# A third accumulator buffer in the gate stages, and GpSimd products moved one stage earlier, in a hashed attention followed by a gated MLP

## The chip, the core and the metric

The kernel runs on one core of one Trainium2 chip. The core has a matrix engine (TensorE, here PE, with its weight loads PEld), a vector engine (VectorE, DVE), an activation engine (ScalarE, ACT), GpSimd (POOL) and a queue engine (SyncE, SP) that issues most DMAs. All of them share the on-chip memory SBUF; PE writes its results to eight accumulator banks (PSUM), from which DVE and ACT read. The metric is the time of one execution in microseconds (us), lower is better.

## The reference

Four batches of eight heads, 768 positions of 64 numbers. Each query and key row gets a bucket: the signs of six projections. Attention is taken only between rows of the same bucket. The result, as 3,072 tokens of 512 numbers, goes through a gated MLP with a gated residual.

```python
q_bits = (np.einsum('bhsd,dk->bhsk', q, proj) > 0)          # 6 bits; k likewise
mask = q_bucket[:, :, :, None] == k_bucket[:, :, None, :]
scores = np.where(mask, scale * q @ k.T, -1e9)
attn = softmax(scores) @ v                                  # then x: 3072 x 512
g = x @ w_gate;  val = x @ w_val                            # 512 -> 1536
ffn_out = gelu(g) * val @ w_out                             # 1536 -> 512
out = x + sigmoid(x @ w_res) * ffn_out
```

## The kernel before

The work is staged by batch. An attention stage of batch b ("a0" to "a3") handles its four pairs of heads (pairs 4b to 4b + 3) in 36 slots, nine a pair. In a slot PE computes 1,024 columns of scores into a two-bank buffer `sp` (L500), ACT takes the exponential `e` (L511), and two slots later PE multiplies the values (L475). In a1 to a3 the MLP of the batch before runs between: residual gate `rps` (L557, then `th` on ACT, L561) in bank `r`, and the output `fps` (L571, then two DVE instructions, L574 and L577, and a store) in bank `f`, six token tiles of 16 matmuls each.

Between two attention stages stands a gate stage ("g0" to "g3"): twelve blocks m, in each of which PE computes the gate half and the value half, eight matmuls each, into one `sp` buffer each (L525). ACT takes the gelu of the first (`gt`, L542), and DVE multiplies it by the second into `hh` (L545). There are two `sp` buffers, so a buffer comes back after two halves. The banks `r` and `f` hold nothing of the gate stage: `hs` (hash sums) uses `r` at its start, and the projection's results use both in the attention stages.

The mask is built without comparing: `nat` holds, for each row of q and k, its 64 numbers (the cast, L261 to L265) and six bits as ±0.5 (L305 or L344). It is transposed into `aug`, by PE in the beginning and by a DMA transposition of SP later (`turn`, L360), so that one matmul gives score and bits together. The bits come in one of two ways. By hash: DVE transposes blocks of 32 (`tr`, L273), PE multiplies by the projection into `hs` (L284), DVE transposes back (L292 into bank `f`, or L296 into SBUF as `ht`), and `bits` compares with zero, four instructions on DVE or POOL. By sums: POOL multiplies the rows by one projection column, one half of a pair at a time (`product`, L335, 12 for each of q and k of a pair), DVE adds up each (`add_up`, L341), and POOL compares (`bits_sums`, L344). Product buffers are shared: in gate stages with `th` (two buffers), in attention stages with `gt` (two buffers).

Every engine works its own list strictly in order. The order comes from lists in the code. `PLAN` lists a0's steps; in the slots of a1 to a3 and after the blocks of the gate stages, pieces hang at places: `('a', b, slot)` or `('g', b, block)`. `PLACES` gives the place of each product; the sum of the product two before stands just ahead of it; `LAYS` gives the place of `bits_sums` and the transposition. Pairs 10, 11, 14 and 15 go by sums, with products from a1 on; 4 to 9, 12 and 13 by hash. At a pair's head a preset matmul (L450) and a DVE copy (`repeat`, L454) initialise the accumulator `av`, and after its last value the `finish` (L419, L420) makes `x_tok`. `x_sb` is its transposition, on which the next gate stage's matmuls work; for the last pair of a batch it is issued (L428) at the very end of the attention stage.

Of the kernel before, what the change touches and what calls it, by code (L numbers as in the profile page):

```python
# [29 lines left out]
    ('vs', 0), ('load', 4, 0), ('load', 5, 1), ('load', 4, 1), ('load_v', 3),  # L30
# [57 lines left out]
XDMA = 2
# [4 lines left out]
def kernel(  # L93
# [12 lines left out]
    nc = tc.nc  # L106
# [14 lines left out]

    LDX, TRX, CSX = 9, 26, 26
    LDY = {1: [('a', 1, 0), ('a', 1, 0), ('a', 1, 3), ('a', 1, 1)], 2: [('a', 2, 0), ('a', 2, 2), ('a', 2, 19), ('a', 2, 19)]}
    CSY = [(5, 's'), (5, 's'), (10, 's'), (10, 's')]
    PLACES = {1: [('a', 1, 9), ('a', 1, 10), ('a', 1, 10), ('a', 1, 11), ('a', 1, 13), ('a', 1, 15), ('a', 1, 15), ('a', 1, 16), ('a', 1, 17), ('a', 1, 18), ('a', 1, 18), ('a', 1, 21), ('a', 1, 22), ('a', 1, 23), ('a', 1, 24), ('a', 1, 26), ('a', 1, 27), ('a', 1, 30), ('a', 1, 34), ('g', 1, 0), ('g', 1, 0), ('g', 1, 0), ('g', 1, 1), ('g', 1, 2), ('g', 1, 3), ('g', 1, 3), ('g', 1, 4), ('g', 1, 5), ('g', 1, 5), ('g', 1, 6), ('g', 1, 6), ('g', 1, 7), ('g', 1, 7), ('g', 1, 8), ('g', 1, 8), ('g', 1, 9), ('g', 1, 9), ('g', 1, 10), ('g', 1, 10), ('g', 1, 11), ('a', 2, 2), ('a', 2, 3), ('a', 2, 5), ('a', 2, 6), ('a', 2, 8), ('a', 2, 9), ('a', 2, 13), ('a', 2, 14)], 2: [('a', 2, 1), ('a', 2, 2), ('a', 2, 13), ('a', 2, 14), ('a', 2, 16), ('a', 2, 18), ('a', 2, 19), ('a', 2, 23), ('a', 2, 24), ('a', 2, 24), ('a', 2, 26), ('a', 2, 31), ('a', 2, 32), ('a', 2, 33), ('g', 2, 0), ('g', 2, 0), ('g', 2, 0), ('g', 2, 0), ('g', 2, 1), ('g', 2, 2), ('g', 2, 3), ('g', 2, 3), ('g', 2, 4), ('g', 2, 5), ('g', 2, 5), ('g', 2, 6), ('g', 2, 6), ('g', 2, 7), ('g', 2, 8), ('g', 2, 8), ('g', 2, 9), ('g', 2, 9), ('g', 2, 10), ('g', 2, 10), ('a', 3, 0), ('a', 3, 4), ('a', 3, 4), ('a', 3, 4), ('a', 3, 6), ('a', 3, 7), ('a', 3, 8), ('a', 3, 13), ('a', 3, 13), ('a', 3, 14), ('a', 3, 14), ('a', 3, 15), ('a', 3, 15), ('a', 3, 16)]}
    DRAIN = {1: ('a', 2, 16), 2: ('a', 3, 20)}
    LAYS = {1: [('g', 1, 7), ('g', 1, 8), ('a', 2, 5), ('a', 2, 17)], 2: [('g', 2, 7), ('g', 2, 8), ('a', 3, 6), ('a', 3, 21)]}
    PRS = (1, 8)  # L130
    NE = 9
    C = 2048.0
    ALPHA = C / np.sqrt(D)
# [196 lines left out]
    def product(x, n, tag):  # L330
        bit, hi = divmod(n, 2)
        if x not in sums:
            sums[x] = hh_pool.tile([P, HT, NBITS], FP32, tag=f"sums{x[0] % 2}{x[1]}", name="sums")
# [460 lines left out]
```

## Time and profile before

| | us |
|---|---|
| median of 3 runs (lowest, highest) | 339.43 (339.25, 339.55) |
| the profiled execution's own time | 339.34 |
| its span, first to last instruction | 337.3 |
| a0 (start to the first gate matmul) | 0 to 45.2 |
| g0 | 45.2 to 78.7 |
| a1 | 78.7 to 121.8, with gate block 0 begun to 126.5 |
| g1 | 126.5 to 157.4 |
| a2, g2, a3, g3 and the last projection | to 205.2, 235.9, 284.3, 313.3, 337.3 |

Times in the rows are counted from the span's start. A row of the timeline gives start, length, engine, line, operation, tiles, shapes and count; in brackets stands the idle time before it and what ended it. A row of the groups gives busy time, mean in nanoseconds, then idle time before and its releasers. A row of waits gives total, times and longest. Rows of engines that end in q are of their queue. Consecutive instructions of one engine overlap a little, so that their starts tell more than their lengths.

### The profile page before, as it was taken

To read this page: it belongs to the slowest core of one execution; us is meant where nothing else is said; L and a number is where in the kernel's file an instruction comes from. 1 tells how busy PE (TensorE), PEld (TensorE's weight loads), DVE (VectorE), ACT (ScalarE), POOL (GpSimd) and SP (SyncE) were. 2 spreads that over 40 slices of the span, in tenths; PEclk is the share of its full clock that TensorE was granted. 3 is DMA by queue.
4 is the path that set the end of the run, shared out by engine and by line. 5 is a ranking of instruction groups with operands and counts; after the bars stand their busy time and mean duration, and the time that the engine had idled before them with its cause. 6 is when DMAs were issued, how large, how long until landed. Compare 5 with 4: busy or idle time off the path is not lost.

```text
span 337.3 us, 7740 instructions
## 1 busy us (share of the span) xinstructions
PE 332.4 (99%) x3086; PEld 204.0 (60%) x3086; DVE 216.3 (64%) x458; ACT 213.8 (63%) x247; POOL 175.0 (52%) x260
## 2 busy tenths in 40 slices
PE   8999999999999999999999999999999999999996
PEld 7767665565666655565666665665566665666444
DVE  7977575554577958876577896876577444343243
ACT  4889962337999952437999982255999984322220
POOL 4779920235299943578799972567879100000000
PEclk9999999999999999999999999999999999999999
DMA  7998999999965223518068933825050340000012
GB/s 228 370 289 125 217 242 202 179 166 205 313 222 149 72 85 81 109 32 187 3 167 229 273 92 94 134 47 96 1 126 33 80 101 33 31 2 0 31 64 94
DMA packets 74387, 43.88 MB, mean 130 GB/s; under 512 B 52544, under 2 KB 71360, under 8 KB 74352
## 3 DMA queue, kind: packets, MB, share of 16 engines
q1 hardware_dynamic: 67872, 37.95, 45.3%
q0 software_dynamic: 6400, 5.44, 10.7%
q8 instruction: 24, 0.39, 0.5%
q14 instruction: 11, 0.09, 0.1%
q10 hardware_dynamic: 80, 0.00, 0.0%
HBM read 29.56 MB, written 6.29 MB: 106 GB/s over the span
## 4 chain that ended last, share of the span: by engine, by line
PE 83%; POOL 8%; ACT 4%; DVE 3%; issue 1%; DMA 1%; POOLq 0%; DVEq 0%; ACTq 0%
PE sp L525 37%; PE fps L571 14%; PE sp L500 14%; PE av L475 7%; PE rps L557 5%; POOL pr L335 4%; PE hs L284 3%; ACT ering L511 3%; ACT e L511 1%; PE wps L229 1%; PE pt L373 1%; POOL v L394 1%; DMA x_sb<-x_tok 1%; DVE sums L341 1%; POOL va L386 1%
## 5 line engine op out<-in xcount | busy, mean ns | idle before, releaser
L511 ACT ACTIVATE e<-sp 128x1024 bf16<-128x1024 f32 x117 | 117.7, 1027 | 8.6 <-PE sp L500 3.7
L335 POOL TENSOR_TENSOR pr<-ld,projr 128x384 f32<-128x384 f32 x96 | 93.8, 998 | 47.0 <-DVE sums L341 31.9
L542 ACT ACTIVATE gt<-sp 128x768 bf16<-128x768 f32 x48 | 38.9, 810 | 83.7 <-PE sp L525 80.0
L500 PE MATMUL sp<-aug,aug 71*128 71x256 bf16 (+1 forms) x384 | 86.0, 325 | 0.5
L571 PE MATMUL fps<-wo,hh 128*128 128x512 bf16 (+2 forms) x312 | 79.6, 362 | 0.0
L545 DVE TENSOR_TENSOR hh<-gt,sp 128x768 bf16<-128x768 bf16 x48 | 45.8, 954 | 42.9 <-PE sp L525 39.5
L525 PE MATMUL sp<-x_sb,wg 128*128 128x512 bf16 (+1 forms) x384 | 70.9, 326 | 0.0
L525 PE MATMUL sp<-x_sb,wv 128*128 128x512 bf16 (+1 forms) x384 | 70.9, 326 | 0.0
L475 PEld LDWEIGHTS <-e 128*128 128x128 bf16 x936 | 43.5, 97 | 25.9
L341 DVE TENSOR_REDUCE sums<-pr 128x6 f32<-128x384 f32 x96 | 50.2, 542 | 10.8 <-POOL pr L335 10.3
L525 PEld LDWEIGHTS <-wg 128*128 128x128 bf16 x384 | 37.1, 98 | 25.8 <-issue 1.5
L525 PEld LDWEIGHTS <-wv 128*128 128x128 bf16 x384 | 37.5, 98 | 24.9 <-issue 0.2
L475 PE MATMUL av<-va,e 128*128 128x65 bf16 x936 | 47.0, 193 | 0.0
L571 PEld LDWEIGHTS <-hh 128*128 128x128 bf16 x312 | 28.1, 97 | 21.6
L500 PEld LDWEIGHTS <-aug 71*128 71x128 bf16 x384 | 29.2, 97 | 11.6 <-issue 2.7
L574 DVE SCALAR_TENSOR_TENSOR fps<-th,fps 128x512 f32<-128x512 f32 (+2 forms) x26 | 17.0, 653 | 25.9 <-PE fps L571 25.8
L557 PE MATMUL rps<-wr,x_sb 128*128 128x512 bf16 x96 | 27.1, 379 | 0.0
L511 ACT ACTIVATE ering<-sp 128x1024 bf16<-128x1024 f32 x27 | 25.8, 1031 | 1.7 <-PE sp L500 1.4
L561 ACT ACTIVATE th<-rps 128x512 f32<-128x512 f32 x24 | 14.3, 594 | 18.7 <-PE rps L557 17.5
L273 DVE STREAM_TRANSPOSE t<-ld 128x768 f32<-128x768 f32 (+3 forms) x28 | 23.1, 843 | 1.7 <-DMA ld<-in_q_dram 1.0
L454 DVE COPY av<-av 128x390 f32<-128x390 f32 x24 | 13.6, 565 | 14.6 <-PE av L450 14.5
L263 POOL TENSOR_SCALAR nat<-ld 128x768 bf16<-128x768 f32 (+1 forms) x12 | 9.6, 804 | 19.3 <-DMA aug<-nat 17.4
(76 smaller groups left out, 257.4 us busy)
## 6 DMA issues: line engine op xcount, KB each, us to landing
ldv<-in_v_dram SPq DMA_DIRECT2D x16, 384.0 KB, 5.8
out_dram<-o SPq DMA_DIRECT2D x23, 256.0 KB, 2.3
ld<-in_q_dram SPq DMA_DIRECT2D x15, 384.0 KB, 5.6
ld<-in_k_dram SPq DMA_DIRECT2D x15, 384.0 KB, 5.8
wg<-in_moe_w_gate_dram POOLq DMA_DIRECT2D x4, 384.0 KB, 9.9
wv<-in_moe_w_val_dram POOLq DMA_DIRECT2D x4, 384.0 KB, 10.7
wo<-in_moe_w_out_dram POOLq DMA_DIRECT2D x3, 512.0 KB, 7.6
wr<-in_moe_w_res_dram POOLq DMA_DIRECT2D x1, 512.0 KB, 16.6
```

The lines of the kernel that those rows point to most:

```text
L273: nc.vector.transpose(t32[p, side][:, sl].rearrange("p c h n -> p (c h n)"), raw[p, side][:, sl].rearrange("p c d -> p (c d)"))
L335: nc.gpsimd.tensor_mul(pr, raw[x][:, hi * T:(hi + 1) * T], projr[:, bit].unsqueeze(1).to_broadcast([P, T, D]))
L341: nc.vector.reduce_sum(sums[x][:, hi * T:(hi + 1) * T, bit], pr, axis=mybir.AxisListType.X)
L475: nc.tensor.matmul(av[p, hi][:, qt, :], e[:, off:off + P], va[:, hi, jt, 0:D + 1], start=first, stop=(repeats(p, hi) and jt == T - 1), ski ...
L500: nc.tensor.matmul(sp[:, off:off + nq * P], ks[0:KA, hi * T + jt, :], qs[0:KA, hi * T + qt0:hi * T + qt0 + nq, :], start=True, stop=True)
L511: nc.scalar.activation(e, sp, AF.Exp, scale=float(ALPHA))
L525: nc.tensor.matmul(sp[:, c0:c1], w[:, kk, bass.ts(m, P)], xs[:, kk, c0:c1], start=(kk == 0), stop=(kk == KM - 1))
L542: nc.scalar.activation(gt, sp[:, 0:S], AF.Gelu)
L545: nc.vector.tensor_mul(hidden[b][:, m, :], gt, ps[1][:, 0:S])
L557: nc.tensor.matmul(rps, x_sb[b][:, kk, t, :], wr[:, kk, :], start=(kk == 0), stop=(kk == KM - 1))
L571: nc.tensor.matmul(fps[:, cs], hh[:, m, bass.ts(t, P)], wo[:, m, cs], start=(m == 0), stop=(m == KF - 1))
L574: nc.vector.scalar_tensor_tensor(fps[:, cs], th[:, cs], 1.0, fps[:, cs], op0=ALU.add, op1=ALU.mult)
```

## The change

- `THIRD` and `gv_parts`: from the fourth block of g0 on and from the third of g1 and g2, every third half goes to banks `r` and `f` (512 and 256 columns) instead of an `sp` buffer. Gelu or product of such a half are two instructions. There are 20 such halves in the three stages, 11 gates and 9 values. g3 is as before.
- The pairs by sums are 7, 10, 11 and 13 (`BY_SUMS`) instead of 10, 11, 14 and 15. Their 96 products begin in g0 and end in a2. Pair 8 is hashed with 6 in g0, 9 with 12 in g1, 14 with 15 in g2.
- The projection columns for the products (`load_rows`, `spread_rows`) are prepared in a0 instead of a1.
- `tokens` always goes to SBUF (`ht`, and `hu` for pair 6's), never to bank `f`.
- Loads, block transposes, casts, bits, weight DMAs and DMA transposes have new places, all in one list `WORK`. Casts of 6, 8, 9, 10, 11 and some others go to ACT, some in attention stages (8,1 at slot 5 and 10,0 at slot 33 of a1; 13,1 at the end of a2). Three weight DMAs stand after block 0 of g0, ahead of the products; seven stand behind bits and products. ("8,1" is the k side of pair 8.)
- `projs` shares the buffers of `th`.

```diff
+WORK = [
+    ('g', 0, 8, 'w'), ('g', 0, 0, 'w'), ('g', 0, 0, 'w'), ('g', 0, 5, 'w'), ('g', 0, 1, 'w'),
+    ('g', 0, 0, 'w'), ('g', 0, 6, 'w'), ('g', 0, 1, 'w'), ('g', 0, 2, 'w'), ('g', 0, 7, 'w'),
...
+    ('a', 1, 3, 'load', 10, 0), ('a', 1, 1, 'load', 10, 1), ('a', 1, 4, 'load', 12, 0),
...
+    ('g', 1, 2, 'cast', 9, 1, 's'), ('a', 1, 33, 'cast', 10, 0, 's'), ('g', 1, 0, 'cast', 10, 1, 's'),
...
+]
+THIRD = {0: 6, 1: 4, 2: 4}
+HASHED = {1: (9, 12), 2: (14, 15)}
+BY_SUMS = (7, 10, 11, 13)
+PLACES = [
+    ('g', 0, 0), ('g', 0, 0), ('g', 0, 1), ('g', 0, 2), ('g', 0, 2), ('g', 0, 2), ('g', 0, 4),
...
+    ('a', 1, 32), ('a', 1, 34), ('g', 1, 0), ('g', 1, 0), ('g', 1, 0), ('g', 1, 0), ('g', 1, 0),
...
+]
+LAYS = [
+    ('a', 1, 0), ('a', 1, 15), ('a', 1, 34), ('g', 1, 7), ('a', 2, 15), ('a', 2, 6), ('g', 2, 2),
+    ('g', 2, 0),
+]
+DRAIN = ('a', 2, 35)
...
-    projs = const.tile([P, 2, P], FP32, name="projs")
+    projs = g_pool.tile([P, 2, P], FP32, tag="th", name="projs")
...
+    def gv_parts(wide=False):
+        if wide:
+            return [(mm_ps.tile([P, 512], FP32, tag="r", name="gvr"), 0, 512),
+                    (mm_ps.tile([P, S - 512], FP32, tag="f", name="gvf"), 512, S)]
+        sp = sc_ps.tile([P, 1024], FP32, tag="sp", name="sp")
+        return [(sp[:, 0:512], 0, 512), (sp[:, 512:S], 512, S), (sp[:, 0:S], 0, S)]
...
                 else:
-                    sp = gv_mm(b, m, w, 0, KM)
+                    n = 2 * m + i - THIRD.get(b, 2 * KF)
+                    parts = gv_mm(b, m, w, 0, KM, gv_parts(n >= 0 and n % 3 == 0))
...
+                whole = parts[2:] or parts
                 if w is wg:
                     gt = g_pool.tile([P, S], BF16, tag="gt", name="gt")
-                    nc.scalar.activation(gt, sp[:, 0:S], AF.Gelu)
+                    for ps, c0, c1 in whole:
+                        nc.scalar.activation(gt[:, c0:c1], ps, AF.Gelu)
...
-            nc.vector.tensor_mul(hidden[b][:, m, :], gt, ps[1][:, 0:S])
+            for ps, c0, c1 in whole:
+                nc.vector.tensor_mul(hidden[b][:, m, c0:c1], gt[:, c0:c1], ps)
...
+    for where, b, i, name, *args in WORK:
+        if name != "hash":
+            put(where, b, i, lambda name=name, args=args: STEP[name](*args))
+    spread_out([(p, side) for p in BY_SUMS for side in range(2)], PLACES, DRAIN, LAYS)
```

More of the change, by code (lines that the diff above doesn't have):

```diff
@@ L651, in spread_out @@
             put(*p, lambda y=y: bits_sums(y), lambda y=y: turn(*y))
-    for b in range(B - 1):
-        s0, p0 = b * NSLOT, (b + 1) * HP
-        xs = [(p0 + i, side) for i in range(2) for side in range(2)]
-        ys = [(p0 + 2 + i, side) for i in range(2) for side in range(2)]
-        if b == 0:
-            continue
-        for j, x in enumerate(xs):
-            loads(s0 + LDX + 3 * j, (x[0], "qk"[x[1]]))
-            at(s0 + TRX + 2 * j, lambda x=x: tr(*x))
-            at(s0 + CSX + 2 * j, lambda x=x: cast(*x, nc.gpsimd))
-        gv(b, 0, lambda p0=p0: tokens((p0, p0 + 1), True))
-        for m, x in zip((0, 1, 2, 4), xs):
-            lay(b, m, x)
-        for y, (where, bb, i) in zip(ys, LDY[b]):
-            put(where, bb, i, lambda y=y: load(y[0], y[1]))
-        for y, (m, eng) in zip(ys, CSY):
-            gv(b, m, lambda y=y, eng=eng: cast(*y, ENG[eng]))
-        spread_out(ys, PLACES[b], DRAIN[b], LAYS[b])
-    at(NSLOT + PRS[0], load_rows)
-    at(NSLOT + PRS[1], spread_rows)
     for p in range(HP, NPAIR):
@@ L703, in first_gv @@
     def first_gv(i):
-        begun.append(gv_mm(0, 0, (wg, wv)[i], 0, KM - 1))
+        begun.append(gv_mm(0, 0, (wg, wv)[i], 0, KM - 1, gv_parts()))
     STEP = dict(
@@ L721 @@
         w=load_w, load=load, load_v=load_v, xturn=lambda hp: x_turn(0, hp),
-        gelu=gelu_table, gv=first_gv)
-    for m, name, *args in BESIDE_GV:
-        gv(0, m, lambda name=name, args=args: STEP[name](*args))
+        gelu=gelu_table, gv=first_gv, rows=load_rows, spreadrows=spread_rows)
+    for where, b, i, name, *args in WORK:
+        if name != "hash":
+            put(where, b, i, lambda name=name, args=args: STEP[name](*args))
+    spread_out([(p, side) for p in BY_SUMS for side in range(2)], PLACES, DRAIN, LAYS)
     for name, *args in PLAN:
@@ L749 @@
             gelu_table()
-            begun = [gv_mm(b, 0, w, 0, KM - 1) for w in (wg, wv)]
+            begun = [gv_mm(b, 0, w, 0, KM - 1, gv_parts()) for w in (wg, wv)]
             if b < B - 1:
                 mlp_mm(NMM)
-                gate_val(b, begun, lambda: hashed(ps))
+                gate_val(b, begun, lambda: hashed(HASHED[b]) if b in HASHED else None)
             else:
```

48 lines of the change are left out of this document (16 added, 32 removed), and 60 rows, old and new, of tables (PLACES, PLAN, WORK).

## The prediction

> **What bounds the kernel now.** I read the page's busy shares first, then busy time by stage, then the chain, then the seams where the chain leaves TensorE. The shares:
>
> ```profile
> PE 332.4 (99%) x3086; PEld 204.0 (60%) x3086; DVE 216.3 (64%) x458; ACT 213.8 (63%) x247; POOL 175.0 (52%) x260
> ```
>
> TensorE (PE) is busy 332.4 of 337.3 us. Busy is modelled, so I check the pace of starts (rows of the chain in order of time: start, length, what):
>
> ```profile
> 128.81 28.72 PE sp L525 x176
> ...
> 314.15 2.59 PE fps L571 x12
> ```
>
> Twelve 512-column matmuls in 2.59 us are 0.216 us each. In g1 176 matmuls take 28.72 us, 0.163 each, 2.61 us a gate block of 16. Eight of them (four of 512, four of 256) take 1.30 us. So a gate stage already runs at the matmul's own pace, and removing a wait there gains only what is left as a gap. Busy time by stage (a1, g1, a2, g2, a3; bounds, length, then busy and count by engine):
>
> ```profile
> 78.70:126.50 47.80, 47.77 (x502) 28.69 (x500) 31.35 (x69) 41.34 (x45) 33.72 (x49) 1.00 0.64 175
> 126.50:157.40 30.90, 30.85 (x214) 18.51 (x213) 24.73 (x48) 12.97 (x17) 18.44 (x20) 1.00 0.46 88
> 157.40:205.20 47.80, 47.66 (x503) 28.90 (x501) 33.64 (x72) 41.35 (x45) 39.14 (x56) 1.00 0.59 159
> 205.20:235.90 30.70, 30.70 (x214) 18.39 (x212) 24.64 (x48) 12.95 (x17) 18.40 (x20) 1.00 0.49 87
> 235.90:284.30 48.40, 48.40 (x511) 29.37 (x509) 26.14 (x58) 42.28 (x47) 23.52 (x36) 1.00 0.27 65
> ```
>
> The third, fifth, sixth and seventh numbers are PE, DVE, ACT and POOL, then comes the granted clock, 1.00 throughout. PE fills every stage; DVE, ACT and POOL have room. The change leaves PE's work alone: both programs have 5,868 instructions on it, the same matmuls, 20 of the 96 gate and value results going to other banks. So only PE gaps can be gained. Four seams show them (timeline rows of several engines):
>
> ```profile
> 57.70 1.46 PE L525 MATMUL sp<-x_sb,wg 128*128 128x512 bf16 x8
> 59.19 1.46 PE L525 MATMUL sp<-x_sb,wv 128*128 128x512 bf16 x8
> ```
> ```profile
> 56.24 1.91 DVE L305 TENSOR_SCALAR nat<-ht 32x72 bf16<-32x72 f32 x8
> 58.18 0.95 DVE L545 TENSOR_TENSOR hh<-gt,sp 128x768 bf16<-128x768 bf16 x1
> ```
> ```profile
> 79.98 0.38 PE L571 MATMUL fps<-wo,hh 128*128 128x512 bf16 x1
> 80.39 0.59 PE L500 MATMUL sp<-aug,aug 71*128 71x256 bf16 x3
> ```
> ```profile
> 77.34 2.01 DVE L305 TENSOR_SCALAR nat<-htp 32x72 bf16<-32x72 f32 x8
> 79.38 0.95 DVE L545 TENSOR_TENSOR hh<-gt,sp 128x768 bf16<-128x768 bf16 x1
> ```
> ```profile
> 160.60 0.41 PE L475 MATMUL av<-va,e 128*128 128x65 bf16 x8
> 161.16 0.59 PE L500 MATMUL sp<-aug,aug 71*128 71x512 bf16 x2
> ```
> ```profile
> 159.59 0.60 ACT L561 ACTIVATE th<-rps 128x512 f32<-128x512 f32 x1 [0.20 <-DVE sums L341]
> 160.09 3.89 ACT L511 ACTIVATE e<-sp 128x1024 bf16<-128x1024 f32 x4
> ```
>
> Seam 1, g0: eight matmuls from 57.70 are issued by 59.00, the next starts at 59.19: 0.19 lost. It needs the bank that the product of 58.18 frees, and that waited behind eight bits instructions. Seam 2, a1's start: one matmul after 79.98 ends its pitch at 80.20, the next starts at 80.39: 0.19, again a product (79.38 to 80.33) behind bits. Seam 3, a2's start: eight value matmuls (0.03 each) end at 160.85, the next starts at 161.16: 0.31. The exponentials are late because th, whose buffer is shared with the GpSimd products, waited for sums. Seam 4 is g1's start:
>
> ```profile
> 123.78 2.73 DMA x_sb<-x_tok
> ...
> 126.56 0.81 PE sp L525 x4
> ```
> ```profile
> 123.76 2.75 PE L571 MATMUL fps<-wo,hh 128*128 128x512 bf16 x12
> ```
>
> Twelve matmuls from 123.76 end at 126.35; the next waits for x_sb until 126.56: 0.21.
>
> **The change part by part.** *Third buffer.* With two sp buffers the product of block m must be done 1.30 us after its value matmuls, and takes 0.95, so DVE may be 0.35 late. With a third, each buffer returns after three half blocks: 2.61 us, so 1.66 late. That covers seam 1 (the product ended 59.13, 0.13 past 59.00): −0.19, between 0 and −0.19. The price: 11 gelus and 9 products become two instructions. Price of the second piece, from
>
> ```profile
> L542 ACT ACTIVATE gt<-sp 128x768 bf16<-128x768 f32 x48 | 38.9, 810 | 83.7 <-PE sp L525 80.0
> L561 ACT ACTIVATE th<-rps 128x512 f32<-128x512 f32 x24 | 14.3, 594 | 18.7 <-PE rps L557 17.5 <-DVE sums L341 1.1
> L574 DVE SCALAR_TENSOR_TENSOR fps<-th,fps 128x512 f32<-128x512 f32 x23 | 16.0, 694 | 25.2 <-PE fps L571 25.1
> ```
>
> On ACT a line through 594 ns for 512 columns and 810 for 768 puts 256 at 378: 0.594 + 0.378 − 0.810 = +0.16. On DVE the line through 694 (512) and the product's 954 (768) puts 256 at 434: +0.17. Both are estimates; the ends are nothing and the whole second piece. Some 20 × 0.17 = 3.3 us, all beside PE, since g1 leaves ACT 18 us and DVE 6 us idle. Uncovered once: in g1 and g2 the last gelu is split, and the table load and first exponential stand behind it; 0.16 late against seam 3's room. I take 0.
>
> *Products and sums.* 96 of each before and after. By the lists of places the products stand 0, 19, 21, 22, 20, 14 in g0, a1, g1, a2, g2, a3 before, and 19, 25, 26, 26, 0, 0 after; each sum follows two products later.
>
> ```profile
> L335 POOL TENSOR_TENSOR pr<-ld,projr 128x384 f32<-128x384 f32 x96 | 93.8, 998 | 47.0 <-DVE sums L341 31.9
> L341 DVE TENSOR_REDUCE sums<-pr 128x6 f32<-128x384 f32 x96 | 50.2, 542 | 10.8 <-POOL pr L335 10.3
> ```
> ```profile
> DVE sums L341 <- POOL pr L335: 10.3, 16, 3.3
> ```
>
> g1 on DVE: 5 more sums × 0.542 = +2.7, 11 fewer bits × 0.24 (1.91 / 8) = −2.6, three split products × 0.17 = +0.5: 24.7 becomes 25.3 of 30.9. POOL: 5 × 0.998 more, 18.4 to 23.4, and one cast and three bits, to about 25. a1 on DVE: 6 × 0.542 and seven bits × 0.24 more: 31.4 to 36.3 of 47.8. All of it fits beside PE.
>
> Seam 2 goes: the bits that stood before the last product of g0 stand elsewhere (−0.19). Seam 3 goes if th waits only for the first leftover sum: its product has run by then, so the sum ends 0.95 + 0.54 after PE's g1 work (128.81 + 28.72 = 157.53), at 159.0, ahead of 159.59 (−0.31). Each lies between 0 and its whole gap. Against them: a sum that waits for its product holds up DVE's queue, with the presets' copies and the banks' products behind it. Today such waits are 10.3 us in 16 (last row above), the longest 3.3, nearly all free. From 0 to +3.3; I take 0, as DVE keeps 11 us free in a1.
>
> *Row load, spread and weights.* In a0 POOL now issues the row load and spreads it, ahead of two casts:
>
> ```profile
> 39.18 0.83 POOL L248 DMA_DIRECT2D wg<-in_moe_w_gate_dram  x1
> ...
> 83.04 0.87 POOL L355 COPY projr<-pr 128x384 f32<-128x384 f32 x1 [1.89 <-DMA pr<-in_proj_dram]
> ```
> ```profile
> 47.57 0.57 DVE L296 STREAM_TRANSPOSE ht<-hs 128x384 f32<-128x384 f32 x1
> ```
> ```profile
> L305 POOL TENSOR_SCALAR nat<-ht 32x72 bf16<-32x72 f32 x7 | 3.2, 456 | 2.3 <-DVE ht L296 1.8
> ```
> ```profile
> wv<-in_moe_w_val_dram POOLq DMA_DIRECT2D x4, 384.0 KB, 10.7
> ```
>
> An issue costs at most 0.83 (first row), the spread 0.87: the casts and the weights behind them come 1.7 later, and the transposes that need the casts wait for ht (48.1) anyhow: nothing on the path. Seven weight DMAs stood in one run from 39.18; now three do, and seven stand behind bits and products. The second value slice leaves at 39.18 + 1.7 + 0.83 = 41.7, lands by 52.4 and is needed at 57.70 − 1.30 = 56.4. The third leaves behind five bits and two products: 48.1 + 5 × 0.46 + 2 × 1.00 = 52.4, lands by 63.1, and is needed in block 6, at 57.70 + 2 × 2.61 + 1.30 = 64.2. Hidden with 1.1 us to spare; beyond that a us costs a us.
>
> *Loads, casts, transposes.* Four loads move into SP's idle time at the end of a0, and the transposes are spread anew, most of them well ahead of their pair. One, (10,0), stands on SP at slot 34 of a1, behind a load and a v load and ahead of an output store and the last x_sb of batch 1. It waits for GpSimd's bits behind that slot's product, whose buffer is freed by the sum that stands at 118.96 today:
>
> ```profile
> 118.96 0.50 DVE L341 TENSOR_REDUCE sums<-pr 128x6 f32<-128x384 f32 x1
> ...
> 123.20 0.56 DVE L420 TENSOR_TENSOR x_tok<-av,rec 128x384 bf16<-128x384 f32 x1
> ```
> ```profile
> L360 SPq DMA_TRANSPOSE aug<-nat x26: 1274/1439/4151, 27.4 to 262.9; - x26
> ...
> DMA to landing us min/median/max: 3.6/3.8/9.2
> ```
>
> 118.96 + 0.50 + 1.00 + 0.46 = 120.9. SP is busy with it for 1.44 us, to 122.4, and x_tok is ready at 123.76, so x_sb is issued on time; the transposition lands 3.8 us after its issue, at 124.7, when x_sb's has begun. Its cast, now on ACT behind exponential 33 (0.81, as the gelu of as many columns), delays the two last exponentials, whose values PE takes two slots after them: hidden. Seam 4 stays: 0 taken, from −0.21 to +3.8 (x_sb behind a whole one).
>
> [...]
>
> **Sum.** −0.19 − 0.19 − 0.31 = −0.69 on the profiled execution's own 339.34 us (span 337.3 and 2.0 around it): 338.65. That execution lies 0.09 under the median of the runs, 339.43; the difference is less than I can tell, and I say 338.7.
>
> **Rivals.** (1) Gaps only move: another late thing stands behind each, as e behind th. For: the seams are a few tenths wide. Time 339.4. (2) Slower: the transposition of (10,0) is issued after 122.3 (1.4 us later than I reckon), and SP is still at it when x_tok is ready. From there each us costs PE one, up to 3.8. For: POOL has more products in a1. Against: 1.4 us of room. 338.7 plus 1 to 3.8: 339.7 to 342.5, say 341. (3) Slower: sums block DVE in a1 or a2 in front of a preset or a product of the bank; two to three lengths of a product, 338.7 + 2 to 3: 340.7 to 341.7. For: the 10.3 us above, and 6 sums more. Against: 11 us of DVE stay free in a1. [...]
>
> **How the numbers follow.** Forecast 0.52, its own range 338.2 to 339.1; rivals 0.20, 0.13, 0.12, 0.03. 0.2% of the median is 0.68 us, about what a measurement here can tell from no change. Of the forecast 0.40 lies under 338.75, 0.12 above. Faster 0.40, same 0.12 + 0.20 = 0.32, slower 0.13 + 0.12 + 0.03 = 0.28. Range 338.2 to 341.0: half of rivals 2 to 4, 0.14, lies above it, and 0.05 below. The bounds of the seams alone reach from 338.4 (seam 4 gone too) to 339.4.
>
> **What would show it.** Right: no gaps of PE near 59, 80.2 and 161, gate stages of 28.7 us, sums of a3 gone. Wrong: SP's transposition ahead of g1 issued after 122.3 and PE idle before the last matmuls of block 0; a product hh ending over 2.6 us after its value matmuls; the sums' wait for products well over 10.3 us with the preset behind it; bits of 0.5 us and more.

## The result, and the profile after

| | before | after |
|---|---|---|
| median of the runs (lowest, highest), us | 339.47 (339.25, 339.55) | 349.32 (348.04, 349.82) |
| profiled execution's own time | 339.34 | 349.82 |
| its span | 337.3 | 348.1 |

The ratio is 1.0283, 95% interval 1.0258 to 1.0308: 2.8% slower, where 338.7 was forecast, and outside the range. Ratios here leave out executions that took over 1.5% more than the fastest of their kernel, so they can differ a little from the ratio of the medians given. First the page's shares of the changed kernel, then PE's busy tenths and its granted clock in 40 slices of 8.7 us.

```profile
PE 335.0 (96%) x3086; PEld 205.7 (59%) x3086; DVE 212.3 (61%) x448; ACT 218.3 (63%) x264; POOL 179.3 (52%) x273
...
PE   9999999559999999999999999999999999999996
...
PEclk9999999859999999999999999999999999999999
```

PE's busy time grew by 2.6 us, its span by 10.8. Two slices, 61 to 78, have holes, and there the clock fell. By stage (g0, a1, g1, a2, g2, a3; columns as in the prediction), and below it g0 of the kernel before:

```profile
45.40:90.00 44.60, 36.11 (x244) 20.75 (x241) 26.09 (x52) 14.62 (x23) 28.25 (x37) 0.89 1.23 183
90.00:137.70 47.70, 47.69 (x502) 28.89 (x501) 36.00 (x81) 42.28 (x47) 39.38 (x56) 1.00 0.77 178
137.70:168.70 31.00, 30.98 (x213) 18.55 (x213) 25.03 (x46) 14.17 (x22) 26.40 (x30) 1.00 0.35 82
168.70:216.10 47.40, 47.40 (x502) 28.81 (x500) 36.49 (x81) 41.90 (x46) 40.72 (x59) 1.00 0.57 139
216.10:246.90 30.80, 30.80 (x214) 18.47 (x212) 14.14 (x25) 11.85 (x19) 8.09 (x16) 1.00 0.37 61
246.90:295.20 48.30, 48.30 (x510) 29.42 (x508) 20.17 (x48) 42.38 (x47) 2.80 (x6) 1.00 0.28 65
```
```profile
45.20:78.70 33.50, 33.47 (x234) 19.91 (x232) 20.60 (x49) 11.41 (x16) 6.55 (x9) 1.00 1.21 185
```

g0 takes 44.6 instead of 33.5 us: +11.1. All the rest together is 0.3 shorter. So the whole loss lies in one stage, the one in which the products were new. Its hole, in rows of the timeline of several engines, and with it the link of the chain that leads there:

```profile
65.25 0.27 PE L570 MATMUL gvf<-x_sb,wg 128*128 128x256 bf16 x1
72.03 1.97 POOL L345 TENSOR_SCALAR nat<-ht 32x72 bf16<-32x72 f32 x4 [10.15 <-DMA aug<-nat]
72.03 0.84 ACT L301 ACTIVATE nat<-ld 128x768 bf16<-128x768 f32 x1 [11.10 <-DMA aug<-nat]
72.78 0.79 ACT L588 ACTIVATE gt<-sp 128x768 bf16<-128x768 f32 x1
...
73.61 0.95 DVE L592 TENSOR_TENSOR hh<-gt,sp 128x768 bf16<-128x768 bf16 x1 [10.28 <-ACT gt L588]
73.63 2.72 PE L570 MATMUL sp<-x_sb,wv 128*128 128x512 bf16 x8 [8.10 <-ACT gt L588]
```
```profile
55.08 16.87 DMA aug<-nat
```

Read from the bottom row of the first fence upwards. PE stands from 65.36 (65.25 and its pitch of 0.11) to 73.63, 8.27 us, for a bank that a gelu had not read. That gelu stood on ACT behind the cast of (6,0). The cast writes `nat` buffer 0, and the DMA transposition of (4,0) still read it: issued at 55.08, it landed 16.87 us later, at 71.95. GpSimd stood at the same buffer with its bits of (6,0). By the rows, DVE's product and PE stood behind ACT.

The second loss follows from the first. Windows of 4 us, with the granted clock in the sixth column behind the length:

```profile
64.00:68.00 4.00, 1.53 (x10) 0.84 (x9) 0.00 (x0) 0.00 (x0) 0.00 (x0) 0.98 1.37 156
68.00:72.00 4.00, 0.00 (x0) 0.00 (x0) 0.00 (x0) 0.00 (x0) 0.00 (x0) 0.50 1.29 197
72.00:76.00 4.00, 2.37 (x8) 1.06 (x8) 1.51 (x2) 2.30 (x4) 3.70 (x7) 0.50 0.90 184
76.00:80.00 4.00, 4.00 (x20) 2.13 (x19) 2.66 (x5) 0.81 (x1) 3.95 (x6) 0.74 0.95 117
```

After the hole PE runs at half clock until 78.1. The eight matmuls from 73.63 and the eight from 76.14 take 2.51 and 2.27 us to the next start instead of 1.30: 2.18 us. 8.27 + 2.18 is 10.45 of the 10.8. A smaller gap, 0.47 at 46.8, stood behind DVE's block transposition of (8,0), which waited 1.21 for its load.

The transpositions issued between 50 and 72 us, before (the first two rows) and after:

```profile
L360 SPq DMA_TRANSPOSE aug<-nat x5: 1433/1828/4151, 57.3 to 70.6; - x5
...
DMA to landing us min/median/max: 3.8/4.2/9.2
```
```profile
L400 SPq DMA_TRANSPOSE aug<-nat x4: 1600/5526/7930, 51.8 to 71.1; - x4
...
DMA to landing us min/median/max: 3.8/11.3/16.9
```

The median from issue to landing went from 4.2 to 11.3 us. One issue held SP itself 5.5 us instead of 1.8 in the median (the figures behind the count are min/median/max in ns), so that the next one left late too.

The 16.87 us of (4,0) are not all its own. SP's DMAs share one queue, q1 (67,872 packets and 37.95 of the 43.89 MB on the page), and ahead of (4,0) stood (5,0), issued at 51.78 behind the loads of pair 9 (landed at 55.40) and itself landed only at 64.10. From 55.4 to 64.1 the queue sent (packets, MB, share):

```profile
q1 hardware_dynamic: 1665, 0.42, 67.7%
```

One transposition has 1,568 packets (last section), so hardly any of (4,0)'s went before (5,0) was done: some 9 us it waited for (5,0), and 7.85 us later it landed.

### The profile page after: what moved, and what is told of

It reads as the page before. It is cut to its first block, busy times and chain, and to the rows that moved or that the text cites. A ratio compares the mean times of both kernels' runs of the same rounds, so it can differ in the third digit from the quotient of the medians.

```text
span 348.1 us, 7761 instructions
## 1 busy us (share of the span) xinstructions
PE 335.0 (96%) x3086; PEld 205.7 (59%) x3086; DVE 212.3 (61%) x448; ACT 218.3 (63%) x264; POOL 179.3 (52%) x273
## 2 busy tenths in 40 slices
DMA packets 74388, 43.89 MB, mean 126 GB/s; under 512 B 52544, under 2 KB 71360, under 8 KB 74352
## 3 DMA queue, kind: packets, MB, share of 16 engines
q1 hardware_dynamic: 67872, 37.95, 45.9%
## 4 chain that ended last, share of the span: by engine, by line
PE 88%; DMA 8%; DVE 3%; issue 0%; ACT 0%; SPq 0%; DVEq 0%; ACTq 0%
PE sp L570 27%; PE fps L618 18%; PE sp L540 16%; PE av L515 9%; PE rps L604 6%; DMA aug<-nat 5%; PE gvr L570 4%; DMA ld<-in_q_dram 3%; PE gvf L570 2%; PE hs L324 2%; PE pt L413 1%; DVE t L313 1%; PE hs L358 1%; PE wps L269 1%; DVE x_tok L460 0%
## 5 line engine op out<-in xcount | busy, mean ns | idle before, releaser
L588 ACT ACTIVATE gt<-sp 128x768 bf16<-128x768 f32 x37 | 30.0, 811 | 65.3 <-PE sp L570 65.3
L570 PE MATMUL sp<-x_sb,wv 128*128 128x512 bf16 (+1 forms) x312 | 59.0, 331 | 8.1 <-ACT gt L588 8.1
L592 DVE TENSOR_TENSOR hh<-gt,sp 128x768 bf16<-128x768 bf16 x39 | 37.1, 952 | 47.5 <-PE sp L570 34.3
L381 DVE TENSOR_REDUCE sums<-pr 128x6 f32<-128x384 f32 x96 | 50.5, 542 | 11.1 <-POOL pr L375 10.7
L570 PE MATMUL sp<-x_sb,wg 128*128 128x512 bf16 (+1 forms) x296 | 55.8, 330 | 0.1
L540 PEld LDWEIGHTS <-aug 71*128 71x128 bf16 x384 | 29.2, 97 | 11.1 <-issue 2.0
L621 DVE SCALAR_TENSOR_TENSOR fps<-th,fps 128x512 f32<-128x512 f32 (+2 forms) x26 | 16.9, 652 | 27.7 <-PE fps L618 27.6
L434 POOL TENSOR_TENSOR v<-ldv 128x384 f32<-128x384 f32 x16 | 16.0, 999 | 27.5 <-DMA ldv<-in_v_dram 27.2
L608 ACT ACTIVATE th<-rps 128x512 f32<-128x512 f32 x24 | 14.3, 595 | 17.4 <-PE rps L604 17.4
## 6 DMA issues: line engine op xcount, KB each, us to landing
wv<-in_moe_w_val_dram POOLq DMA_DIRECT2D x4, 384.0 KB, 13.3
```

The source lines that it names most:

```text
L381: nc.vector.reduce_sum(sums[x][:, hi * T:(hi + 1) * T, bit], pr, axis=mybir.AxisListType.X)
L540: nc.tensor.matmul(sp[:, off:off + nq * P], ks[0:KA, hi * T + jt, :], qs[0:KA, hi * T + qt0:hi * T + qt0 + nq, :], start=True, stop=True)
L570: nc.tensor.matmul(ps, w[:, kk, bass.ts(m, P)], xs[:, kk, c0:c1], start=(kk == 0), stop=(kk == KM - 1))
L588: nc.scalar.activation(gt[:, c0:c1], ps, AF.Gelu)
L592: nc.vector.tensor_mul(hidden[b][:, m, c0:c1], gt[:, c0:c1], ps)
L621: nc.vector.scalar_tensor_tensor(fps[:, cs], th[:, cs], 1.0, fps[:, cs], op0=ALU.add, op1=ALU.mult)
```

## The experiments

Time is in us, with the ratio to the kernel before on the same chip. Every kernel computes the whole reference.

**Where the wait stands: e1 and e2.** Theory: a late transposition stops whichever engine stands first behind it.

```diff
- ('g', 0, 4, 'cast', 6, 0, 's')
+ ('g', 0, 4, 'cast', 6, 0, 'p')            # e1
```


> The changed kernel, with one letter changed: the cast of (6,0) at block 4 of g0 is GpSimd's again, as before the change. Theory (a DMA transposition that lands 17 us late, whichever engine stands behind it): the wait moves to GpSimd, which then reaches it near 62 and stands until about 72; the products behind it, their sums and the products of the banks on DVE come late by about one block less than in the changed kernel. PE still stands for 4 to 7 us before 74, median 344 to 348. Rival (only the place on ACT is at fault, GpSimd hides the wait as before): no stall over 1 us, median 338.3 to 340.

Measured: 348.96 (347.82 to 351.06), 1.0267 [1.0220, 1.0313]. GpSimd now waits for the transposition, and DVE for GpSimd:

```profile
69.48 0.83 POOL L303 TENSOR_SCALAR nat<-ld 128x768 bf16<-128x768 f32 x1 [7.94 <-DMA aug<-nat]
```
```profile
73.38 0.56 DVE L381 TENSOR_REDUCE sums<-pr 128x6 f32<-128x384 f32 x1 [8.42 <-POOL pr L375]
```

PE stands 6.9 us, against 4 to 7 expected, and the median is just above the range. The engine that casts is not the cause.

```diff
- ('g', 0, 4, 'cast', 6, 0, 's'), ('g', 0, 4, 'bits', 6, 0, 'p'), ('g', 0, 7, 'turn_dma', 6, 0)
+ ('g', 0, 8, 'cast', 6, 0, 's'), ('g', 0, 8, 'bits', 6, 0, 'p'), ('g', 0, 8, 'turn_dma', 6, 0)   # e2
```


> The changed kernel, with the cast, the bits and the transposition of (6,0) moved from blocks 4, 4 and 7 of g0 to block 8; the DMAs before it stay. Theory (the cost is the wait of this one cast with the gelus behind it): the transposition of (4,0) still takes 14 us or more to land, but nothing waits for it; no stall of PE over 1 us in g0, the granted clock stays at 1.00, median 338.4 to 339.7. Rival (another instruction waits next for the late transpositions, such as the cast of (7,1) at block 8 or the bits of (6,1) at block 7): a stall of 2 to 6 us later in g0, median 341 to 346.

Measured: 347.9, 355.5, 357.7 and 358.3 in four runs, median 356.62. My theory missed. The rival had the right kind of wait, but even the shortest run lies above its 341 to 346, and PE stood 10.9 and 4.3 us instead of 2 to 6. The trace is of the run of 358.3; what the shorter ones met isn't shown. In it, with (6,0) out of the way, GpSimd ran ahead and issued `wr` and two `wo` slices from 64.5, beside the transposition of (4,1), issued at 61.31. That one landed at 82.58, 21.3 us later, and DVE's bits of (6,1) waited for it:

```profile
82.67 0.91 DVE L345 TENSOR_SCALAR nat<-ht 32x72 bf16<-32x72 f32 x4 [12.55 <-DMA aug<-nat]
```

Until then the waits of GpSimd had kept the last weights away from the transpositions (in the changed kernel `wr` left at 75.98). Taking away a wait let loose the traffic behind it.

**Which traffic: e3, e4, e5.**

```diff
- ('g', 0, 1, 'w'), ('g', 0, 1, 'w'), ('g', 0, 2, 'w')
+ ('g', 0, 0, 'w'), ('g', 0, 0, 'w'), ('g', 0, 0, 'w')                     # e3, e5
- ('g', 0, 0, 'load', 9, 0), ('g', 0, 0, 'load', 9, 1)
+ ('a', 1, 0, 'load', 9, 0), ('a', 1, 0, 'load', 9, 1)                     # e4, e5
```


> The changed kernel, with the three weight DMAs of blocks 1, 1 and 2 of g0 issued with the other three after block 0, as before the change. Theory A (the transposition is late because weight DMAs run beside it): the last of the six weights lands by 62 to 65 and the transposition of (4,0), issued near 55, 3 to 8 us earlier than in the changed kernel, at 64 to 69; the stall shrinks to 1 to 5 us, median 341 to 346. Theory B (loads on SP's own queue make it late): landing stays near 72 and the stall near 8 us, 348 to 350.

> The changed kernel, with the two loads of pair 9 moved from block 0 of g0 to slot 0 of a1. They carry 0.79 MB, about 3 us of the rate of 274 GB/s seen at 48 to 52. Theory A (weight DMAs beside the transposition): the weights issued before them land up to 3 us sooner, those issued at 53.7 to 57.5 by 1 to 3 us; the stall falls from 8 us to 5 to 7, median 345 to 349. Theory B (loads on SP's queue): the transposition of (4,0) lands by 63, no stall over 1 us, 338.4 to 340.

> The changed kernel, with the two loads of pair 9 in slot 0 of a1 and the three weight DMAs of blocks 1, 1 and 2 after block 0, both edits of the two runs before together. Theory (any DMA traffic beside a transposition makes it late, whichever queue it is on; the two effects add): the six weights land by 61 to 64, the transposition of (4,0) by 58 to 64; the cast at 61 waits 0 to 3 us, PE stands 0 to 1 us, median 339 to 341. Rival (the effects do not add, since what counts is only the traffic at the moment of issue): (4,0) lands near 65 as with the loads moved alone, a stall of 1 to 2 us stays, 341 to 342.5.

| | after | e3 | e4 | e5 |
|---|---|---|---|---|
| median | 349.32 | 345.71 | 341.91 | 342.78 |
| ratio | 1.0283 | 1.0172 [1.0139, 1.0205] | 1.0051 [1.0023, 1.0080] | 1.0087 [1.0063, 1.0110] |
| (4,0) issued | 55.08 | 55.14 | 53.53 | 55.45 |
| last weight issued by then (e4: 0.01 later), landed | 68.72 | 67.11 | 62.35 | 62.34 |
| (4,0) lands | 71.95 | 68.33 | 64.80 | 64.31 |
| PE stands | 8.3 | 4.8 | 1.3 | 1.1 |

The landings are read from the trace, DMA by DMA. With less traffic on either queue beside it (4,0) landed earlier, by 3.6 us in e3 and 7.15 in e4. It lands 1.2 to 3.2 us after the last weight issued by the time of its own issue (in the changed kernel one more, issued at 57.53, landed at 71.47, just before it). The loads of pair 9 count twice: without them (5,0) landed at 56.76 instead of 64.10, and the weight of 53.5 at 62.35 instead of 66.48. (5,0) passed its gain on to (4,0) behind it on the queue. For e3 theory A held and B fell. For e4 neither did, but B, the loads on SP's own queue, came nearer: (4,0) at 64.8 where it said by 63, and a stall of 1.3 where it said at most 1; theory A had taken 1 to 3 us off the stall, and 7 went. In a1 of e4 PE then waited 2.2 us for late `wo`. In e5 (4,0) landed at 64.3, at the end of the theory's 58 to 64 and near the rival's 65; stall and median are the rival's, and e5 is no faster than e4.

**The same, put into the kernel before: e8.** The loads of pairs 8 and 9 stand in block 0 of g0 instead of slots 9 to 18 of a1; nothing else differs.

> The kernel before, with one thing added: the loads of pairs 8 and 9 (1.57 MB in four DMAs) stand after block 0 of g0 instead of in slots 9 to 18 of a1, so that weights and loads are still under way when the transpositions of pairs 4 and 5 are issued from 57. Theory (a transposition is slowed by whatever other DMAs run beside it): those transpositions take 8 to 17 us instead of 4.0 to 4.4, the casts on GpSimd and the bits of (6,0) behind them on DVE come late, median 340 to 346. Rival (the slow transpositions come from how the changed kernel orders its own queues, not from traffic): 4 to 5 us each, median 339.2 to 340.

Measured: 341.91 (339.25 to 346.41), 1.0049 [1.0016, 1.0082]. The five transpositions issued from 58.1 to 71.3 take 8.2, 5.9, 3.8, 4.1 and 10.6 us; three of them shorter than I expected; the weights had landed by 65. Still GpSimd's first cast waited 21.2 us instead of 17.4, and the `wo` DMAs behind it left 4.0 us later:

```profile
86.35 0.38 PE L571 MATMUL fps<-wo,hh 128*128 128x512 bf16 x1 [1.55 <-DMA wo<-in_moe_w_out_dram]
```

Traffic alone makes the kernel before slower, by 0.5%: again late transpositions hold a cast, and what stands behind the cast comes late. Here that is a weight.

**All waits out of the way: e6, e9, e11, e12, e15, e16.** Each takes e5's edits (e11 only the loads') and moves what the trace of the last one showed waiting. Their edits to the changed kernel, in short:

```diff
# e6: as e5; cast and bits of (6,0) at block 6, bits of (6,1) at block 9
# e9: as e5, but loads of pair 9 in slots 6, 8 of a1; only the cast at block 6; ('tr', 8, 0) behind the last finish
# e11: e9 with three weights left in blocks 1, 1, 2
# e12: e6 with those loads; the last four 'w' in blocks 7, 7, 8, 9; load (10,0) in slot 0; ('tr', 8, 0) behind the last x_sb
# e15: e12; last four 'w' behind bits of (6,0), blocks 6, 6, 7, 8; turn of (6,1) in slot 5 of a1; tr of (8,0) and (8,1) exchanged
# e16: e15; casts of (8,0), (8,1) in slots 3, 12 of a1, their bits in 4, 13; turn of (6,1) in slot 2, load (10,0) in slot 1
```


> As the run before, and the cast and the bits of (6,0) at block 6 instead of 4, the bits of (6,1) at block 9 instead of 7, so that nothing stands in a queue for a transposition before 66. Theory (only waits for late transpositions, and weights that are late in their turn, cost time in g0): no stall of PE over 0.4 us between 48 and 80, median 338.3 to 339.6, about as fast as the kernel before or a little faster. Rival (GpSimd, no longer held up, issues the last weights earlier, and they make the next transpositions late, as when the cast alone was moved): a stall of 1 to 5 us between 70 and 95, 340.5 to 345.

> The changed kernel with four edits: six weight DMAs after block 0 of g0 (as two runs before), the two loads of pair 9 in slots 6 and 8 of a1 (behind the loads of pair 10, whose product waited 1.4 us when pair 9 stood in slot 0), the cast of (6,0) on ACT at block 6 instead of 4 while GpSimd's bits of (6,0) stay at block 4, and the block transposition of (8,0) on DVE behind the last finish of batch 0. Theory (a transposition lands 0.5 to 2 us after the last weight DMA that was under way when it was issued; GpSimd, held by its bits until then, sends the last weights after the transpositions): the six weights land by 63, (5,0) and (4,0) by 65, the next ones in 3.8 to 5 us; no stall of PE over 0.4 us from 45 to 100, median 338.2 to 339.6 with the kernel before at 339.4 to 339.8. Rival (some other wait takes the place, as in the two runs in which the cast was moved): a stall of 1 us or more, 340.5 or more.

> The four edits without the first: three of the six weight DMAs stay in blocks 1, 1 and 2 of g0, behind bits and products. Theory (transposition lands just after the weights issued before it): (5,0) by 58, (4,0) near 65, (5,1) and (4,1) after the last of the three weights, near 69 to 71; GpSimd's bits hold until 65 and the cast at block 6 lands in time; 338.5 to 341. Rival (the three late weights alone make the stall): a stall of 2 us or more and 341.5 or more.

> The changed kernel with the six weight DMAs after block 0 of g0 and the last four at blocks 7, 7, 8 and 9 instead of 5, 6, 7 and 8; the loads of pair 9 in slots 6 and 8 of a1, that of (10,0) in slot 0; cast and bits of (6,0) at block 6, bits of (6,1) at block 9; the block transposition of (8,0) behind the last copy of x_sb. So weights, transpositions and the last weights come one after the other, and no instruction stands in front of a transposition that is under way. Theory (all of the loss lies in these waits): weights landed by 63, four transpositions by 70, no stall of PE over 0.4 us from 45 to 100, median 338.2 to 339.6. Rival (the 19 products and sums, or the casts on ACT, cost DVE and ACT more than g0 has): gaps of 0.3 us and more in several blocks, 340.5 or more.

> The run e12 with three edits: the last four weight DMAs right behind GpSimd's bits of (6,0) (blocks 6, 6, 7 and 8; about 2 us sooner), the transposition of (6,1) in slot 5 of a1 instead of 0 (so that it does not run beside the last two), and the block transpositions of (8,0) and (8,1) changed in order, so that DVE meets (8,0) only after its load has landed. Theory (the trace of e12: 1.5 and 1.2 us of PE in a1 go to late wo slices, 0.6 at 48 to a late hash): wo landed by 84, no PE gap over 0.4 us from 45 to 100, median 338.3 to 339.2 with the kernel before at 339.4 to 339.9. Rival (another wait again): a gap of 1 us or more between 70 and 95, 340 or more.

> The run e15 with the waits taken away that its trace shows: the cast of (8,0) in slot 3 of a1 (bits in slot 4) instead of block 10 of g0, the cast of (8,1) in slot 12 (bits in 13) instead of 5 and 11, the transposition of (6,1) in slot 2 instead of 5, the load of (10,0) in slot 1 instead of 0, so that it does not run beside the last weights. Theory (all loss lies in instructions that stand behind late DMAs): no PE gap over 0.4 us from 45 to 100 except up to 1 us for wo slices near 82 to 86, median 338.3 to 339.6 with the kernel before at 339.3 to 339.9. Rival (the casts in a1 hold up exponentials, or one more late DMA is met): gaps of 1 us and more, 340.5 or more.

| | median | ratio | what PE stood for, by the trace: us from one matmul's start to the next, less its pitch |
|---|---|---|---|
| e6 | 352.65 | 1.0356 [1.0305, 1.0408] | 5.0 and 3.3: casts on ACT behind (5,1) and (6,0), landed 13.3 and 18.3 after issue |
| e9 | 342.64 | 1.0073 [1.0049, 1.0097] | 2.5: sums behind GpSimd's bits, which waited 4.4 for (4,0) |
| e11 | 341.46 | 1.0034 [1.0002, 1.0066] | 4.0 in the profiled run (345.08): the same wait; runs from 339.16 |
| e12 | 341.97 | 1.0072 [1.0056, 1.0089] | 3.1 in a1 for `wo`, 0.8 at 48 for a hash; nothing else in g0 |
| e15 | 347.66 | 1.0233 [1.0218, 1.0248] | 1.9 and 4.5: casts on ACT behind (6,0) and (6,1) |
| e16 | 339.47 | 1.0002 [0.9987, 1.0017] | 0.7 in a1 for `wo`, 0.4 at 80 for g0's last product |

In e6, e9, e11 and e15 my theory missed each time, since another instruction met a late DMA; in e12 it held for g0, but for the hash, and missed in a1. Each run carries several edits, so most of them show only that the wait moves. Of one transposition, that of (6,0), the pair e12 and e15 shows the cause most cleanly, first e12, then e15:

```profile
L400 SPq DMA_TRANSPOSE aug<-nat x1: 1432/1432/1432, 69.1 to 69.1; - x1
...
DMA to landing us min/median/max: 3.7/3.7/3.7
```
```profile
L400 SPq DMA_TRANSPOSE aug<-nat x1: 1433/1433/1433, 69.0 to 69.0; - x1
...
DMA to landing us min/median/max: 10.2/10.2/10.2
```
```profile
68.95 0.84 POOL L288 DMA_DIRECT2D wr<-in_moe_w_res_dram  x1
69.79 0.76 POOL L288 DMA_DIRECT2D wo<-in_moe_w_out_dram  x1
```

Same issue time, same source, and the transposition ahead of it had landed, or did within 0.5 us (69.60 in e12, 69.06 in e15). In e15 `wr` was issued 0.09 us ahead of it (last fence), in e12 1.95 us behind it, at 71.09: 10.2 against 3.7 us. e16 repeats e15: `wr` 0.08 ahead, 10.5 us. In e12 the cost was moved, not gone: the last weights came later, and PE waited for them in a1. e16 leaves (6,0) late and takes the casts that stood behind it away; it is the first form of the whole change in which PE nowhere stands over 0.5 us from g0 on, and it is as fast as the kernel before. So the loss lay in those waits, and not in the products, sums or split pieces.

**What the third buffer is worth: e7, e10, e13, e14, e17.** e7, e10 and e13 are e6, e9 and e12 with

```diff
- THIRD = {0: 6, 1: 4, 2: 4}
+ THIRD = {}
```


> As the run before, without the third buffer: every half of the gate stages goes to one of the two sp buffers. Theory of the prediction (the third buffer lets DVE be 1.66 us late instead of 0.35, which matters where sums and bits stand before a product of the banks): PE gaps of 0.2 to 1 us come back in several blocks of g0 to g2; 0.3 to 3 us slower than the run before. Rival (DVE is seldom over 0.35 us late, and 20 split gelus or products cost as much as they save): within 0.3 us of the run before.

> The run before without the third buffer. Theory of the prediction (without it DVE may be only 0.35 us late at a product of the banks): gaps of 0.2 to 1.4 us in g0 to g2 as in the earlier run without it (1.3 near 59, 0.8 near 136, 1.3 near 155), 2 to 5 us slower than the run before. Rival (the gaps of that earlier run came from late DMAs): within 0.5 us of the run before.

> The run before without the third buffer. Theory (the products and sums of the gate stages make DVE late by more than 0.35 us in some blocks, and the third buffer covers that): gaps of 0.3 to 1.4 us near 60, 136, 145 and 156 as in both earlier runs without it, 3 to 5 us slower. Rival (these gaps came with late DMAs): within 0.5 us.

Measured: 345.33, 345.71 and 347.21. e7 is faster than e6, which neither of its two theories had; it also met other late DMAs (its (6,0) landed after 9.3 us instead of 18.3), so this pair tells nothing. The other two pairs meet much the same late DMAs: 3.1 and 5.2 us slower without the buffer, as the theory said (2 to 5 and 3 to 5), in e13 with up to 1.7 us of half clock in it (last section). PE's waits for products of the banks, in e13 (in e12 there are none):

```profile
PE sp L570 <- DVE hh L592: 3.3, 5, 1.2
```

e14, run again as e17, is the kernel before with the buffer and what it needs (`gv_parts`, `THIRD`, the hashes of the gate stages in SBUF instead of bank `f`, `projs` in the buffers of `th`).

> The kernel before with the third buffer alone (same blocks as in the changed kernel; the hashes of the gate stages go to SBUF instead of bank f, which the buffer needs). Theory of the prediction: the gap of 0.19 us near 59 goes, the rest stays; 338.9 to 339.5 with the kernel before at 339.4 to 339.8, which these rounds may not tell from no change. Rival (split gelus and products cost more than they free): 0.3 to 2 us slower.

> The kernel before with the third buffer alone, once more. Theory of the prediction: 0.19 us faster (0.05%), which the interval will hold. Alternative: 0.4 to 0.7 us faster (0.1 to 0.2%), as the first run had it, because the buffer also takes up what DVE is late in g1 and g2.

Measured: 339.42, 0.9980 [0.9962, 0.9998], and 339.29, 0.9986 [0.9977, 0.9995]: 0.5 us faster than the kernel before (0.2 to 0.8 by the second interval). In the trace of e17 PE's gap of 0.19 near 59 is gone, that near 80 is down from 0.19 to 0.05 (79.61 + 0.22 to 79.88), and one of 0.11 at 236.7 is new: about 0.2 in all. Where the rest of the 0.5 comes from isn't shown. The size is that of the alternative in the expectation, its reason is not: the gaps that went belong to g0. It is the one version here that is faster than the kernel before.

## Why the prediction was wrong, point by point

**The step that failed** is "Loads, casts, transposes". It said that the transposes are "spread anew, most of them well ahead of their pair", gave them no cost, and, for the one it looked at, a landing of 3.8 us. Two things were wrong in it.

- I asked when a pair needs its transposition, and not who writes its source next. Four `nat` buffers serve all pairs: the cast and bits of (6,0) may write only when (4,0) is out. The cast now stood on ACT ahead of gelus, the bits at block 4 instead of 7 on GpSimd ahead of products. e1, e9 and e11 show the same wait on other engines.
- I took the landing from a median, 3.8. The quoted row also held 9.2, and g0 of the kernel before has a DMA share of 1.21. In the new order (5,0) and (4,0) were issued 5.6 and 2.3 us earlier than the first transposition of the kernel before (51.78 and 55.08 against 57.35), with weights and loads still under way (in the kernel before one weight, landed at 60.23); (4,0) took 16.9. e12 and e15 show 3.7 and 10.2 us at the same place.

Also missed was the clock: 2.2 us lost at 0.50 behind the stall. In the kernel before and in e16, which have no such stall, it stood at 1.00 from 45.2 to 90.

**Weights** were a step that failed in size. The value slice that I let land "by 63.1", with 1.1 us to spare, landed at 66.48: issued at 53.73 instead of 52.4, and 12.75 us under way instead of 10.7. The stall hid it. e12 shows the price where it isn't hidden: 3.1 us for `wo`.

**Third buffer.** The mechanism was right: seam 1 of the kernel before closes. The size was −0.19 and measured −0.5. Seam 2, which I had credited to the moved bits, all but closes too; in e17 the eight bits in front of its product take 1.93 us instead of 2.01, now that they read SBUF (in the kernel before the median is 219 ns from `ht` in SBUF and 228 from `htp` in bank `f`), so not all of that is the buffer's. In the new order, with 19 products in g0, it is worth some 3 us. I had put that at nothing beyond the seam, since the new sums and products fit "beside PE". Free time of the stage didn't help a product of the bank that was late by a sum (PE's 3.3 us of waits in e13).

Prices: a split gelu has rows of 0.60 and 0.38, a split product 0.69 and 0.41. The estimates for the second pieces were 0.378 and 0.434.

**Seams.** Rows of the changed kernel, for seams 1, 2 and 3:

```profile
60.00 0.55 DVE L381 TENSOR_REDUCE sums<-pr 128x6 f32<-128x384 f32 x1 [0.91 <-POOL pr L375]
...
60.47 0.94 DVE L592 TENSOR_TENSOR hh<-gt,sp 128x768 bf16<-128x768 bf16 x1
...
61.11 0.27 PE L570 MATMUL gvf<-x_sb,wv 128*128 128x256 bf16 x1
...
61.47 1.46 PE L570 MATMUL sp<-x_sb,wg 128*128 128x512 bf16 x8
```
```profile
89.13 1.14 PE L570 MATMUL sp<-x_sb,wv 128*128 128x512 bf16 x6
...
90.11 0.60 PE L540 MATMUL sp<-aug,aug 71*128 71x512 bf16 x2
```
```profile
171.80 0.41 PE L515 MATMUL av<-va,e 128*128 128x65 bf16 x8
172.05 0.59 PE L540 MATMUL sp<-aug,aug 71*128 71x512 bf16 x2
```

Seam 1 only moved: 61.11 + 0.11 to 61.47 is 0.25, behind a sum that waited 0.91 for GpSimd. Seams 2 and 3 are gone, as forecast (six matmuls from 89.13 take 0.98, eight from 171.80 take 0.25). Seam 4 stays: 0.19 at 137.7. So the gain was there, about 0.5 us of the 0.69, under a loss twenty times as large. In e16 seam 1 is down to 0.07 and seam 3 is gone, but PE waits 0.37 at seam 2 and 0.7 for `wo`, and its first gate matmul starts at 45.52 instead of 45.22: gains and losses cancel.

**Rivals.** None came in the changed kernel. (1): seam 1 moved, but two seams went; with the stalls taken away, in e16, its 339.4 came (339.47). (2): seam 4 unchanged, no late x_sb. (3): sums waited for products 10.7 us in 21 places, the longest 0.9, where before it was 3.3. The chance of 0.03 stood for bits and products that hold each other up, 2.5 us in five groups; no run shows such a wait. DVE's 62 bits instructions of that shape have a mean of 218 ns in the changed kernel; the ten that lie wholly inside GpSimd's products take 216, the longest 220. The list lacked the rival that a transposition becomes late. The 5,868 instructions on PE, on which "the same matmuls" rests, stand in no trace; both traces have 3,086 matmuls, so the premise holds.

## What to carry to other kernels

Before you move a DMA, or a write to the buffer it reads, list for every buffer the last reader and the next writer, and what stands behind that writer on its engine; cost the reader by what else is under way and by what stands ahead of it in its own queue, not by the median of its rows; here even the slowest row, 9.2, was far below the 16.9. A wait that you remove also releases whatever stood behind it: look at what that will issue. Take the parts of a change apart when they can be: here one part was worth 0.5 us, and the placement of the others cost 10.

## What the runs showed of the hardware

**DMA transpositions beside other DMAs.** Packets of each queue in stretches of the trace: weights alone (kernel before, 46 to 57.3), transpositions nearly alone (before, 57.3 to 67.6), both together (after, 55.4 to 72). q0 is GpSimd's queue, q1 SP's.

```profile
DMA packets 2979, 2.30 MB, mean 204 GB/s; under 512 B 96, under 2 KB 2978, under 8 KB 2978
```
```profile
DMA packets 6536, 1.84 MB, mean 179 GB/s; under 512 B 6288, under 2 KB 6535, under 8 KB 6535
...
q1 hardware_dynamic: 6272, 1.57, 89.9%
```
```profile
DMA packets 5777, 2.36 MB, mean 142 GB/s; under 512 B 4014, under 2 KB 5776, under 8 KB 5776
...
q0 software_dynamic: 1827, 1.35, 76.6%
q1 hardware_dynamic: 3949, 0.99, 63.5%
```

Four transpositions make 6,272 packets of 250 B, 1,568 each; a weight slice of 384 KB comes in packets of about 770 B, so 512. Together both are slow, 142 GB/s against 204 and 179: the bytes of the third stretch would take 1.35 / 0.204 + 0.99 / 0.179 = 12.1 us one after the other, and took 16.6.

How much of each queue went shows in e3 from 56 to 64 us, where a transposition (issued at 55.14, landed at 68.33) and weights (the last landed at 67.11) were under way together:

```profile
q0 software_dynamic: 1391, 1.03, 90.4%
q1 hardware_dynamic: 1384, 0.35, 41.5%
```

The packets are nearly equal in number, 1,391 and 1,384. At such counts a transposition of 1,568 packets takes about as long as three slices of 512, by an estimate from these numbers, and its packets are a third as large: in e3 SP's queue got 0.35 of the 1.38 MB. That fits its landing just after the last of the slices beside it. In the changed kernel the counts are not equal throughout (1,360 of q1 to 127 of q0 from 56 to 60, 522 to 708 from 60 to 66, 1,097 to 843 from 66 to 71), and in the first two stretches 108 and 112 GB/s went in all; what slowed both there stays open.

**The clock after a pause of PE.** In the trace of the changed kernel the granted clock falls to 0.50 at 67.85 and is back at 1.00 at 78.09, 10.24 us later; in that of e13 it falls at 87.22 and is back at 90.63, 3.41 us later, a third of that. Windows of 3.41 us (PE's busy time follows the length, the clock follows GpSimd's), from e13 with a pause of 1.9 us from 84.2, then e15 with one of 1.9 from 78.9, then e9 with one of 2.5 from 69.0:

```profile
83.81:87.22 3.41, 1.70 (x17) 0.92 (x16) 2.33 (x7) 2.07 (x4) 3.41 (x5) 1.00 1.35 131
87.22:90.63 3.41, 3.19 (x24) 1.91 (x24) 0.00 (x0) 2.00 (x2) 3.08 (x8) 0.50 1.18 265
90.63:94.05 3.42, 3.42 (x41) 2.18 (x40) 2.08 (x5) 2.95 (x4) 0.89 (x1) 1.00 1.12 338
```
```profile
77.12:80.53 3.41, 1.99 (x13) 1.08 (x11) 2.61 (x6) 1.30 (x2) 3.12 (x4) 1.00 1.20 239
80.53:83.94 3.41, 3.12 (x16) 1.55 (x16) 2.70 (x6) 3.38 (x5) 3.41 (x4) 1.00 1.23 209
```
```profile
66.72:70.13 3.41, 2.38 (x15) 1.37 (x14) 0.64 (x2) 0.93 (x2) 3.20 (x6) 1.00 0.91 170
70.13:73.55 3.42, 2.04 (x13) 1.26 (x13) 2.62 (x5) 0.54 (x1) 3.38 (x5) 1.00 0.86 115
```

e13's pause lies in one window, with 1.70 us of work, and in the next the clock was 0.50. In the changed kernel the window ahead of the fall, 64.44 to 67.85, has 1.09 us; the three at 0.50 behind it have 0.00, 1.05 and 3.41, and the clock was back after the third. e13's was back after one with 3.19. e15's pause is as long as e13's, its window has 1.99, and the clock stayed at 1.00; e9's longer one is divided between two windows of 2.38 and 2.04, and the clock stayed too. So in these runs the longest of the three pauses was not the one that cost the clock: of the windows given here it fell after those with 1.09 and 1.70 us of PE's work, and not after those with 1.99, 2.04 and 2.38. What decides beyond these windows isn't shown.
